# A speech joint kernel: prompts' products split around the first convolution, and transposes of the first chunk and of four weights moved from TensorE to DMA

## The chip, the cores and the metric

One core of one Trainium2 chip runs the kernel. The metric is the device time of one execution in microseconds (us). Before the change three runs took 842.79, 841.05 and 825.72 us, the median being 841.05. A profiled execution of the same kernel is read below.

## The reference

Forward and backward pass of a small speech model with a joint network. Two batches of 16000 rows of 256 channels go through two strided convolutions with three taps, each followed by a GELU; eight prompts per batch (`g`) are projected; every remaining frame is joined with every prompt by a tanh, and the result is projected again.

```python
h = gelu(conv3(x, w1))[:, ::2, :]          # 16000 -> 8000 rows
f = gelu(conv3(h, w2))[:, ::2, :]          # 8000 -> 4000 rows
fe = jnp.einsum("btd,de->bte", f, w_f)
ge = jnp.einsum("bud,de->bue", g, w_g)
j = jnp.tanh(fe[:, :, None, :] + ge[:, None, :, :])
out = jnp.einsum("btud,dv->btuv", j, w_o)
```

The outputs are `out` and the gradients of all seven inputs (x, w1, w2, g, w_f, w_g, w_o) for a given `grad_out` of shape (2, 4000, 8, 256). All tensors are bfloat16.

## The kernel before

The 4000 frames of both batches, with a gap of 16 between them, make one line of 8016 columns that is cut into 16 chunks of 512 (`G`, the last one shorter). Channels lie on the 128 partitions, in two halves (`KT`). For each chunk n there are:

- `conv_units(n)` (L302): the first convolution. Six matmuls of 512 columns (L324) make one of its four units, ACT copies the result out of PSUM (L327), and the GELU with its derivative is spread over ACT and DVE (L264, L269). `conv2_units(n)` (L342, matmuls L359) is the second convolution; `fe_units(n)` (L374, L383, L385) makes the tile `FE`, of which there is one buffer.
- `tanh(n, u)` (L394): ACT makes `JT`, the joint of chunk n with prompt u, from `FE` and the bias `GE` (L401).
- `joint_units(n, up)` (L675), one step for a pair of prompts. `gj` multiplies the transposed output gradient `GOT` with `WOT` (L635), ACT squares JT (`JSQ`, L627), and DVE combines both to `NGZ` (L639), which POOL adds up over the prompts (`ngfe_acc`, L658). Then `o_block` projects JT with `WO` (L695) and ACT copies the output rows (L697). The gradient of w_o, `gwo` (L734), needs JT with frames on the partitions: the tile `JR`. A step runs `gwo` for the pair before it.
- the backward units of chunk n - 1: `d1_units` reads `WFT` (L431), `d5_units` reads `W2T` (L454), `e_units` reads `W1T` (L590); they are transposed weights. `WGT` is read only at the end (L910).

`JR` comes in two ways. For chunks 1 to 15, `load_jr` (L660) starts a transposing DMA from JT in SBUF (L667). For chunk 0 it only takes the buffer, and `jr_block` (L670) makes it in `joint_units`: four transposes of 128 x 128 on TensorE for each of four blocks (L467), and one DVE copy out of PSUM each (L469).

All other transposed loads (`x` in L164, `GOT` in L174, `FR` in L474) are DMAs on SP's queue too, beside the plain loads `GO` (L202) and the weights. POOL's queue writes the outputs and loads the rows of x.

Before the loop over the chunks, the start runs 16 dummy matmuls (`warm`, L782) on a tile of zeros, then `small_units` (L786), which transposes the prompts (L790) and makes `GE` (L796, L798) one batch after the other, then the convolution of chunk 0, two units of chunk 1's, three units of `transposed_units` (L801: WOT, WFT, WGT), the second convolution, the rest of chunk 1's first convolution, and the six other transposed weights (L813 on TensorE, L814 on DVE). 

`weave` (L747) sets the order in which units are written down: after every unit of a step it draws `ratio` units of a second list, the fill. In chunk 0 `ratio` is 0.4, and the fill holds the second convolution of chunk 1 and its `FE`, with empty units between. A planner then makes one list for each engine and each DMA queue from the program, its dependencies and its own idea of durations, so an instruction may come earlier than its place in the program when nothing holds it. `tc.add_manual_dep(..., NOSYNC)` puts one instruction behind another in that plan without a wait on the chip; `tc.keep_in_program_order` forbids the move. In the trace SP issues the x loads of chunk 2 (second half) and chunk 3 (first half) together at 28.99, although the latter is written down in chunk 1.

Of the kernel before, what the change touches and what calls it, by code (L numbers as in the profile page):

```python
# [22 lines left out]
P = 128  # L23
KT = 2
KK = 3
# [7 lines left out]
def kernel(  # L33
# [106 lines left out]
    W1T = const.tile([P, KK, KT, D], BF16, name="W1T")  # L140
    W2T = const.tile([P, KK, KT, D], BF16, name="W2T")
# [13 lines left out]

    def load_x(n, pairs=(0, 1)):
        W = geom(n)[1]
        for c in pairs:
            t = X1[c] if n == 1 else xcp.tile([P, 2, KT, CW + 16], BF16, name="XC")
            back = 16 * c  # L160
            for lo, hi in gaps(n, back):
                nc.vector.memset(t[:, :, :, 16 + lo:16 + hi], 0.0)
            for b, q, col, w in segs(n, back):
                nc.sync.dma_start_transpose(out=t[:, :, :, 16 + col:16 + col + w].rearrange("p c k w -> p (c k) w"),  # L164
                                            in_=xq[b, c, q:q + w, :])
            for j in range(2):
                S[n]["X", 2 * c + j] = t[:, j]
# [269 lines left out]
    def d5_units(n):  # L437
# [10 lines left out]
        for par, taps in ((0, ((1, 0),)), (1, ((2, -1), (0, 0)))):  # L448
            for mt in range(KT):
                ps = ps_f32()  # L450
                k, last = 0, len(taps) * KT - 1
                for (i, sh) in taps:
                    for kt in range(KT):
                        nc.tensor.matmul(ps[:, :N], lhsT=W2T[:, i, kt, mt * P:(mt + 1) * P],  # L454
                                         rhs=GF[:, kt, 2 + sh:2 + sh + N], start=(k == 0), stop=(k == last))
                        k += 1
                gh = nc.vector.tensor_tensor(out=GH[:, par, mt, 2:2 + N], in0=ps[:, :N],
                                             in1=G1[:, par, mt, 2 - par:2 - par + N], op=ALU.mult)
                while held:
                    tc.add_manual_dep(held.pop().ins, gh.ins.name, NOSYNC, reason="held")  # L460
                yield
# [111 lines left out]
    def e_units(n):  # L573
# [5 lines left out]
        def gx_block(k, M):  # L579
            t = gxp.tile([P, 4, D], BF16, name="GX")  # L580
            combos = (((0, 1, 0), (2, 0, -1)), ((1, 1, 0),), ((2, 1, 0), (0, 0, 0)), ((1, 0, 0),))
            for cp in range(2):
                ps = ps_f32()
                for cj in range(2):
                    cc = combos[2 * cp + cj]
                    j, last = 0, len(cc) * KT - 1
                    for (i, par, sh) in cc:
                        for kt in range(KT):
                            o = 2 + k + sh
                            nc.tensor.matmul(ps[:M, cj * D:(cj + 1) * D], lhsT=GH[:, par, kt, o:o + s * (M - 1) + 1:s],  # L590
                                             rhs=W1T[:, i, kt, :], start=(j == 0), stop=(j == last))
# [68 lines left out]
    def load_jr(n, up):  # L660
# [4 lines left out]
        if n == 0:  # L665
            return
        nc.sync.dma_start_transpose(out=JR[:].rearrange("p u k a d -> p (u k a) d"),  # L667
                                    in_=S[n]["JTP", up][:].rearrange("p u k w -> p (u k w)"))

    def jr_block(n, up, k):  # L670
        o, M = blocks(geom(n)[1])[k]
        srcs = [(S[n]["JT", 2 * up + j][:, kt, o:o + M], 2 * j + kt, M) for j in range(2) for kt in range(KT)]
        transposes(srcs, [(S[n]["JR", up][:M, :, :, k].rearrange("p u k d -> p (u k) d"), M, 0, 4)])

    def joint_units(n, up):  # L675
# [7 lines left out]
        if n == 0:  # L683
            for k in range(len(bl)):
                jr_block(n, up, k)
                yield
# [99 lines left out]
    def small_units():  # L786
        for b in range(B):
            gt = ps_bf()
            for kt in range(KT):
                nc.tensor.transpose(out=gt[:, kt, 0:U], in_=GR8[:, b, kt * P:(kt + 1) * P], identity=ident[:U, :U])  # L790
            gT = gxp.tile([P, KT, U], BF16, name="gT")
            nc.vector.tensor_copy(out=gT[:], in_=gt[:, 0:KT, 0:U])
            ge = ps_f32()
            for mt in range(KT):
                for kt in range(KT):
                    nc.tensor.matmul(ge[:, mt * U:(mt + 1) * U], lhsT=WG[:, kt, mt * P:(mt + 1) * P], rhs=gT[:, kt, :],  # L796
                                     start=(kt == 0), stop=(kt == KT - 1))
            nc.vector.tensor_copy(out=GE[:, b].rearrange("p k u -> p (k u)"), in_=ge[:, 0:KT * U])  # L798
            yield

    def transposed_units():  # L801
        jobs = []
        for WT_, W_ in ((WOT, WO), (WFT, WF), (WGT, WG)):
            jobs.append(([W_[:, dt, kp * P:(kp + 1) * P] for kp in range(KT) for dt in range(KT)],
                         WT_[:].rearrange("p k d -> p (k d)")))
        for WT_, W_ in ((W2T, W2), (W1T, W1)):
            for i in range(KK):
                jobs.append(([W_[:, i, dt, kp * P:(kp + 1) * P] for kp in range(KT) for dt in range(KT)],
                             WT_[:, i].rearrange("p k d -> p (k d)")))
        for srcs, dst in jobs:  # L810
            ps = ps_bf()
            for j, src in enumerate(srcs):
                nc.tensor.transpose(out=ps[:, j, :], in_=src, identity=ident[:])  # L813
            nc.vector.tensor_copy(out=dst, in_=ps[:, 0:4, :].rearrange("p k d -> p (k d)"))  # L814
            yield
# [7 lines left out]
    conv1, turned = conv_units(1), transposed_units()  # L823
    for _ in chain(warm(16), small_units(), conv_units(0), islice(conv1, 2), islice(turned, 3), conv2_units(0)):
        pass
# [7 lines left out]
    for n in range(G):  # L833
# [16 lines left out]
        for up in range(U // 2):  # L850
# [7 lines left out]
            for piece in (((0,), (1,), (2, 3), ()) if n == G - 1 else ((0, 1), (2, 3), (), ()))[up] if back else ():  # L858
                load_xr(n - 1, piece)
            main = joint_units(n, up)  # L860
# [95 lines left out]
```

## Time and profile before

| | before |
|---|---|
| profiled execution | 824.49 us |
| its span, first to last instruction | 822.4 us |
| granted TensorE clock, mean over the span | 0.996 |
| PE busy | 799.5 us, 97% |
| DVE busy | 627.8 us, 76% |
| ACT busy | 678.8 us, 83% |
| POOL busy | 403.4 us, 49% |
| moved by DMA | 187.88 MB, 228 GB/s |
| chain that ended last | PE 84%, ACT 8%, DVE 5% |

PE is TensorE's matmuls, DVE VectorE, ACT ScalarE, POOL GpSimd, SP SyncE. A stage line gives the start and end of the stage, its length, then the busy time of PE, PE's weight loads, DVE, ACT and POOL with the count of instructions in parentheses, the granted clock of TensorE as a share of full speed, the busy share of the 16 DMA engines (over 1 where packets overlap), and GB/s. A group line gives source line, engine, operation, output and inputs with shapes and the count, then busy time and the mean of one in ns, then the idle time of the engine just before them and what ended it. A wait line says who waited for whom: total us, times, longest. A line on DMA issues gives output and input, queue, kind, count, size, and the median us from issue to landing.

### The profile page before, as it was taken

Reading aid. Unit: us, or ns where it says so; the run is one execution under the profiler, and the core shown is the slowest. Engines: PE = TensorE matmul, PEld = TensorE weight load, DVE = VectorE, ACT = ScalarE, POOL = GpSimd, SP = SyncE. Lnnn points to the kernel's source line nnn. Section 1 sums busy time; section 2 is a strip of 40 time slices with the busy share of each in tenths; the row PEclk is TensorE's granted clock in tenths of the full one; section 3 lists DMA queues with packets and bytes.
Section 4 is the critical chain, followed back from the end, with each engine's and each line's share of the span. In section 5 each row is a group of like instructions: output and inputs, shape, how many; then the busy total and the mean of one; then the engine's idle time right before and its main releaser. Section 6 shows DMA issues by size and latency. Waiting matters only on the chain.

```text
span 822.4 us, 16555 instructions
## 1 busy us (share of the span) xinstructions
PE 799.5 (97%) x6292; PEld 596.6 (73%) x6368; DVE 627.8 (76%) x1211; ACT 678.8 (83%) x1080; POOL 403.4 (49%) x423
## 2 busy tenths in 40 slices
PE   8789999999999999999999999999999999999997
PEld 3356777868678687776767778686786867878796
DVE  3996786886869778697877968868697786968744
ACT  4988898896979969799797988969799697987744
POOL 1154644454545534544487544545455345455671
PEclk9999999999999999999999999999999999999999
DMA  9968999999999999999999999999999999999954
GB/s 216 214 172 189 212 258 236 235 220 240 260 270 207 237 229 228 261 231 203 250 232 243 248 225 252 221 250 264 262 222 241 229 241 230 211 200 249 275 135 139
DMA packets 395344, 187.88 MB, mean 228 GB/s; under 512 B 343296, under 2 KB 379032, under 8 KB 395264
## 3 DMA queue, kind: packets, MB, share of 16 engines
q1 hardware_dynamic: 374944, 119.69, 78.2%
q0 software_dynamic: 20320, 67.12, 27.0%
q8 instruction: 50, 0.82, 0.4%
q14 instruction: 30, 0.25, 0.1%
HBM read 51.38 MB, written 50.34 MB: 124 GB/s over the span
## 4 chain that ended last, share of the span: by engine, by line
PE 84%; ACT 8%; DVE 5%; issue 2%; DMA 1%; POOL 0%; POOLq 0%; DVEq 0%; ACTq 0%
PE GWO_ps L734 12%; PE ps L695 11%; PE ps L635 10%; PE ps L590 10%; PE ps L603 10%; PE ps L324 8%; PE ps L530 5%; PE pst L467 5%; PE ps L454 4%; PE ps L359 4%; ACT JT L401 2%; ACT OUT L697 2%; ACT JSQ L627 2%; PE ps L512 2%; PE ps L431 1%
## 5 line engine op out<-in xcount | busy, mean ns | idle before, releaser
L658 POOL TENSOR_TENSOR ACCN<-ACCN,NGZ 128x1024 f32<-128x1024 f32 (+1 forms) x80 | 169.1, 2114 | 74.0 <-DVE NGZ L639 73.0
L639 DVE SCALAR_TENSOR_TENSOR NGZ<-JSQ,ps 128x512 bf16<-128x512 bf16 (+3 forms) x272 | 168.6, 640 | 42.4 <-PE ps L635 32.5
L401 ACT ACTIVATE JT<-FE,GE 128x512 bf16<-128x512 f32 (+3 forms) x272 | 176.9, 707 | 0.5
L697 ACT CAST OUT<-ps 128x512 bf16<-128x512 f32 (+1 forms) x252 | 145.9, 593 | 35.2 <-PE ps L695 35.1
L627 ACT ACTIVATE JSQ<-JT 128x1024 bf16<-128x1024 bf16 (+1 forms) x128 | 134.9, 1058 | 37.2 <-DVE NGZ L639 37.2
L695 PE MATMUL ps<-WO,JT 128*128 128x256 bf16 (+1 forms) x1008 | 148.4, 272 | 2.5 <-DVE NGZ L639 2.1
L734 PE MATMUL GWO_ps<-GO,JR 128*128 128x256 bf16 (+1 forms) x1008 | 149.0, 272 | 0.7
L722 POOL DMA_DIRECT2D out_dram<-OUT x76 | 56.0, 737 | 168.4 <-ACT OUT L697 156.2
L635 PE MATMUL ps<-GOT,WOT 128*128 128x512 bf16 (+1 forms) x482 | 133.1, 374 | 2.4 <-DVE JR L469 0.9
L734 PEld LDWEIGHTS <-JR 128*128 128x128 bf16 (+1 forms) x1008 | 97.1, 98 | 26.1 <-issue 0.5
L695 PEld LDWEIGHTS <-JT 128*128 128x128 bf16 (+1 forms) x1008 | 97.4, 98 | 23.3 <-issue 3.6
L590 PE MATMUL ps<-W1T,GH 128*128 128x256 bf16 (+2 forms) x756 | 100.4, 273 | 0.7
L590 PEld LDWEIGHTS <-GH 128*128 128x128 bf16 (+2 forms) x756 | 83.5, 116 | 13.0
L603 PE MATMUL ps<-rows,XR 128*128 128x256 bf16 (+1 forms) x756 | 90.4, 273 | 0.0
L415 DVE TENSOR_TENSOR ACC<-ACC,ps 128x512 f32<-128x512 f32 x90 | 61.5, 685 | 37.5 <-PE ps L530 25.9
L264 DVE SCALAR_TENSOR_TENSOR g_s<-g_sq,g_x 128x1024 bf16<-128x1024 bf16 (+2 forms) x35 | 67.4, 1925 | 27.0 <-ACT g_sq L264 27.0
L324 PE MATMUL ps<-XC,W 128*128 128x512 bf16 (+1 forms) x359 | 86.9, 380 | 0.7
L603 PEld LDWEIGHTS <-XR 128*128 128x128 bf16 (+1 forms) x756 | 73.9, 98 | 11.6
L593 ACT CAST GX<-ps 128x512 bf16<-128x512 f32 (+2 forms) x126 | 72.2, 587 | 9.7 <-PE ps L590 5.8
L245 POOL DMA_DIRECT2D out_dram<-GX x67 | 36.9, 550 | 81.3 <-ACT GX L593 79.8
L635 PEld LDWEIGHTS <-WOT 128*128 128x128 bf16 x512 | 48.2, 98 | 34.7 <-issue 3.5
L324 PEld LDWEIGHTS <-W 128*128 128x128 bf16 x384 | 37.9, 99 | 39.2 <-issue 2.2
(133 smaller groups left out, 1228.1 us busy)
## 6 DMA issues: line engine op xcount, KB each, us to landing
GO<-in_grad_out_dram SPq DMA_DIRECT2D x56, 512.0 KB, 6.1
out_dram<-OUT POOLq DMA_DIRECT2D x56, 512.0 KB, 6.0
out_dram<-GX POOLq DMA_DIRECT2D x55, 256.0 KB, 5.1
XR<-in_x_dram POOLq DMA_DIRECT2D x39, 256.0 KB, 7.1
XR<-in_x_dram POOLq DMA_DIRECT2D x13, 320.0 KB, 7.2
GO<-in_grad_out_dram SPq DMA_DIRECT2D x4, 384.0 KB, 4.7
out_dram<-OUT POOLq DMA_DIRECT2D x4, 384.0 KB, 5.6
GOT<-in_grad_out_dram SPq DMA_TRANSPOSE x68, 7.8
```

The costliest lines, as they stand in the source:

```text
L324: nc.tensor.matmul(ps[:, :W], lhsT=W1[:, i, kt, mt * P:(mt + 1) * P], rhs=st["X", c][:, kt, 16 + sh:16 + sh + W], start=(k == 0), stop=(k ...
L401: act = nc.scalar.activation(out=JT[:, mt, lo:hi], in_=S[n]["FE"][:, mt, lo:hi], func=ACT.Tanh, bias=GE[:, b, mt, u:u + 1], scale=1.0)
L590: nc.tensor.matmul(ps[:M, cj * D:(cj + 1) * D], lhsT=GH[:, par, kt, o:o + s * (M - 1) + 1:s], rhs=W1T[:, i, kt, :], start=(j == 0), stop=( ...
L593: nc.scalar.copy(out=t[:M, 2 * cp:2 * cp + 2, :], in_=ps[:M, :])
L603: nc.tensor.matmul(ps[:, dt * D:(dt + 1) * D], lhsT=XR[:M, 4 * k + i + 2 * (1 - par), dt * P:(dt + 1) * P], rhs=t[:M, g + 2 * par:g + 2 * ...
L627: jsq = nc.scalar.activation(out=JSQ[:, :, :W], in_=JT[:, :, :W], func=ACT.Square)
L635: nc.tensor.matmul(ps[:, :W], lhsT=WOT[:, kt, mt * P:(mt + 1) * P], rhs=GOT[:, kt, :W], start=(kt == 0), stop=(kt == KT - 1))
L639: nc.vector.scalar_tensor_tensor(out=NGZ[:, mt, lo:hi], in0=JSQ[:, mt, lo:hi], scalar=1.0, in1=ps[:, lo:hi], op0=ALU.subtract, op1=ALU.mul ...
L658: st["last"] = nc.gpsimd.tensor_tensor(out=out, in0=in0, in1=st["NGZ", u][:, :, :W], op=ALU.add)
L695: nc.tensor.matmul(ps[:M, j * V:(j + 1) * V], lhsT=st["JT", u][:, kt, o:o + M], rhs=WO[:, kt, :], start=(kt == 0), stop=(kt == KT - 1))
L697: nc.scalar.copy(out=OUT[:M, k, :], in_=ps[:M, :])
L734: nc.tensor.matmul(GWO_ps[:, dt, :], lhsT=JR[:M, j, dt, k, :], rhs=GO[:M, k, j * V:(j + 1) * V], start=(n_gwo[0] == 0), stop=(n_gwo[0] == ...
```

## The change

1. `small_units` becomes `prompt_units`: its first unit transposes the prompts of both batches into one PSUM tile and copies them out at once; its second makes all of `GE`. The start now runs 12 dummy matmuls, the first unit, 9 dummy matmuls, the convolution of chunk 0, and only then the second unit.
2. `load_jr` starts the transposing DMA for chunk 0 too; `jr_block` and its units in `joint_units` are gone.
3. `transposed_units` keeps `WOT` alone. `WFT`, `W2T`, `W1T` and `WGT` are loaded from HBM by four transposing DMAs (`load_transposed`), written down ahead of the fourth step of chunk 0. W1T and W2T change their layout so that one DMA fills each.
4. `behind` orders SP's queue: the x load of chunk 2 (second half) comes behind the JR load of step 0; that of chunk 3 (first half) and the four weights come behind the JR load of step 2.

```diff
+    def behind(dma, up):
+        tc.add_manual_dep(dma.ins, S[0]["JRD", up].ins.name, NOSYNC, reason="behind the first chunk's tanh rows")
+
...
-                nc.sync.dma_start_transpose(out=t[:, :, :, 16 + col:16 + col + w].rearrange("p c k w -> p (c k) w"),
+                dma = nc.sync.dma_start_transpose(out=t[:, :, :, 16 + col:16 + col + w].rearrange("p c k w -> p (c k) w"),
                                             in_=xq[b, c, q:q + w, :])
+                if (n, c) in ((2, 1), (3, 0)):
+                    behind(dma, 0 if n == 2 else 2)
...
         S[n]["JR", up] = JR
-        if n == 0:
-            return
-        nc.sync.dma_start_transpose(out=JR[:].rearrange("p u k a d -> p (u k a) d"),
+        S[n]["JRD", up] = nc.sync.dma_start_transpose(out=JR[:].rearrange("p u k a d -> p (u k a) d"),
                                     in_=S[n]["JTP", up][:].rearrange("p u k w -> p (u k w)"))
...
-        if n == 0:
-            for k in range(len(bl)):
-                jr_block(n, up, k)
-                yield
...
+    def prompt_units():
+        gt = ps_bf()
         for b in range(B):
             for kt in range(KT):
-                nc.tensor.transpose(out=gt[:, kt, 0:U], in_=GR8[:, b, kt * P:(kt + 1) * P], identity=ident[:U, :U])
+                nc.tensor.transpose(out=gt[:, b * KT + kt, 0:U], in_=GR8[:, b, kt * P:(kt + 1) * P], identity=ident[:U, :U])
+        gT = gxp.tile([P, B * KT, U], BF16, name="gT")
+        nc.vector.tensor_copy(out=gT[:], in_=gt[:, 0:B * KT, 0:U])
+        yield
...
+    def load_transposed():
+        for WT_, w_ in ((WFT, w_f), (W2T, w2), (W1T, w1), (WGT, w_g)):
+            if WT_ in (W2T, W1T):
+                dma = nc.sync.dma_start_transpose(out=WT_[:].rearrange("p k i d -> p k (i d)"), in_=w_.rearrange("i a d -> (i a) d"))
+            else:
+                dma = nc.sync.dma_start_transpose(out=WT_[:], in_=w_)
+            behind(dma, 2)
...
-    for _ in chain(warm(16), small_units(), conv_units(0), islice(conv1, 2), islice(turned, 3), conv2_units(0)):
+    for _ in chain(warm(12), islice(prompts, 1), warm(9), conv_units(0), prompts, islice(conv1, 2), islice(turned, 3),
+                   conv2_units(0)):
...
+            if n == 0 and up == 3:
+                load_transposed()
             main = joint_units(n, up)
```

## The prediction

> **What bounds the kernel now.** I read the busy time by stage first, since a mean over the span mixes a start with a long steady stage.
>
> ```profile
> core 0: us, PE busy (x) PEld busy (x) DVE busy (x) ACT busy (x) POOL busy (x), PEclk, DMA share, GB/s
> 0.00:10.00 10.00, 6.59 (x24) 2.58 (x25) 1.25 (x7) 1.49 (x2) 3.27 (x13) 1.00 0.91 194
> 10.00:20.00 10.00, 9.84 (x46) 4.39 (x47) 5.36 (x16) 6.52 (x13) 0.00 (x0) 0.83 1.06 234
> ...
> 30.00:40.00 10.00, 6.88 (x47) 3.99 (x47) 9.97 (x23) 9.68 (x16) 1.90 (x2) 1.00 1.04 231
> 40.00:50.00 10.00, 8.77 (x67) 5.79 (x67) 10.00 (x21) 9.15 (x15) 5.70 (x6) 1.00 0.45 113
> 50.00:60.00 10.00, 7.16 (x57) 4.96 (x57) 10.00 (x18) 8.45 (x14) 6.87 (x4) 1.00 0.71 186
> 60.00:70.00 10.00, 8.84 (x67) 5.82 (x67) 7.92 (x22) 7.90 (x12) 5.11 (x4) 1.00 0.61 175
> 70.00:810.00 740.00, 735.25 (x5867) 558.26 (x5936) 570.40 (x1076) 620.93 (x989) 377.41 (x391) 1.00 1.09 233
> ```
>
> From 70 to 810 us PE is busy 735.25 of 740. The change removes nothing there: all its edits lie in the first 70 us or are loads. So what it can win is the distance by which that full stage starts earlier, and what it can lose is a new hole at its start. In 30 to 70, PE is busy 31.65 of 40 and DVE 37.9, with ACT at 35.2. The chain of waits through these 40 us alternates between ACT and DVE, mostly ACT (JT, JSQ, OUT). DMA has room in 40 to 70 (0.45, 0.71, 0.61 against 1.09 later).
>
> Second, finer stages around the first convolution, for the granted clock:
>
> ```profile
> 8.00:9.40 1.40, 0.01 (x1) 0.00 (x0) 0.17 (x1) 0.00 (x0) 0.00 (x0) 1.00 1.07 183
> 9.40:10.40 1.00, 0.68 (x11) 0.58 (x12) 0.32 (x3) 0.00 (x0) 0.00 (x0) 0.90 1.28 291
> 10.40:13.60 3.20, 3.20 (x9) 1.09 (x8) 0.16 (x1) 0.60 (x2) 0.00 (x0) 0.50 0.99 214
> 13.60:20.00 6.40, 6.35 (x35) 3.09 (x35) 5.14 (x14) 5.92 (x12) 0.00 (x0) 1.00 1.08 240
> ```
>
> PE is empty from 8.0 to 9.4 (the prompts' products wait for WG), and the clock is 0.50 from 10.4 to 13.6, exactly under the first convolution.
>
> Third, the waits of ACT from 24 to 70 us, the groups of DVE and PE that go, and the landings:
>
> ```profile
> ACT OUT L697 <- PE ps L695: 2.9, 2, 2.0
> ACT g_s L264 <- DVE g_s L264: 1.9, 2, 1.5
> ```
> ```profile
> L469 DVE COPY JR<-pst 128x512 bf16<-128x512 bf16 x16 | 5.9, 410 | 0.0
> L467 PE MATMUL pst<-ident,JT 128*128 128x128 bf16 x64 | 5.2, 218 | 3.6 <-DVE NGZ L639 3.3 <-DVE JR L469 0.3
> ```
> ```profile
> JR<-JT SPq DMA_TRANSPOSE x60, 7.2
> ...
> WG<-in_w_g_dram POOLq DMA_DIRECT2D x1, 128.0 KB, 6.1
> ...
> GR<-in_g_dram POOLq DMA_DIRECT2D x1, 8.0 KB, 4.3
> ```
>
> ACT is idle only 4.8 us of these 46, all of it behind work that the change takes away or that stands in one line with it.
>
> **Part 1, prompts around the convolution.** The 16 dummy matmuls start at 1.81; 12 go at 0.427 us each (their weight loads stand that far apart), to 6.9, the other four at the full rate. Now 12 run, to 6.9; GR is issued at 2.66 and lands 4.3 later, at 7.0; four transposes take some 0.2 us; nine dummies at 0.216 (the pitch after 13.6) take 1.9. The convolution starts at about 9.2 instead of 10.20. Its x: the second pair is issued at 2.2 and lands 7.5 later, at 9.7, before its taps are due; the first pair's landing has no record, at latest 10.2, so the earlier start is worth 0 to 1.0. PE has no hole of 1.4 us before it any more, so I expect clock 1.0: eight matmuls that lie between 10.2 and 13.6 at 0.427 would take 0.216, another 1.7. The first unit ends at 9.2 + 6 x 0.216 = 10.5 and its cast starts at 10.6 instead of 12.96: 2.4 earlier. From there ACT is nearly dense to the first tanh (28.78), so I carry 2.4, between 0.7 (x late, one dummy too many) and 2.7. The moved products (8 small matmuls, about 0.5 us) run behind the convolution, while ACT and DVE make the GELU; GE is needed only at the tanh, 11 us later. Without that cover they would cost 0.5.
>
> The Trainium skill ("TensorE: Matmul & The Clock Gate", Part 1) says that the clock halves after an idle window of about 3.4 us and rises after a busy one. Here a hole of 1.4 us was enough, as the 0.50 row shows, so the measurement decides; by the page's rule no hole this short would matter, the earlier start alone would be left, 1.0 instead of 2.4 us, and the sum would read 821.0.
>
> **Part 2, first chunk's JR by DMA.** Gone are 64 transposes on PE (0.056 apart: 3.6 us) and 16 copies on DVE (0.41 long, 0.33 apart: 5.3 us). PE has holes there, so its 3.6 buy little by themselves; but in each of the four steps the output matmuls L695 stand behind these transposes, which stand behind DVE (3.6 us of waits), and ACT waits 2.9 for L695. Added: four JR transposes on SP. The bound is ACT's own idle time, 4.8 us (2.9 + 1.9); DVE gives back more than that with Part 3. Nothing of the rest of ACT's work is removed. I take 3.0 of the 4.8, because POOL's additions stretch DVE instructions beside them (a 0.68 us multiply took 2.06 at 38.91, 2.56 at 46.64) and will go on doing so; the ends are 0 and 4.8.
>
> The new wait: SP waits for the tanh of both prompts, and behind it in its queue stand GOT, GO and x. GOT has cover: those issued at 50.67 and 61.39 are used by L635 only 20 us later. JR itself is needed by L734. Before, the last tanh of steps 0, 1, 2 ends at 31.9, 40.5, 47.8, and L734 reads at 42.8, 53.1, 62.1: 10.9, 12.6 and 14.4 us. The steps shorten by 1 to 2, so 9 is left at worst, against landings of 4.3 to 12.3, median 7.2: hidden, with 2 us of cover. The fourth JR is read a whole step later.
>
> **Part 3, four weights by DMA.** Gone are 32 transposes on PE (1.8 us) and 8 DVE copies (2.6 at 0.33), six of them between 30.5 and 32.9, just ahead of the NGZ that everything waits for. Their worth is inside the 4.8. Added are 1.05 MB on SP behind the third JR, some 45 to 55 us; WFT is first read at 71.4, W2T at 77.5, W1T at 96.7, WGT at the end. Hidden by 10 us and more.
>
> **Load on DMA.** Two 512 KB transposes back to back took 6.44 us from 17.11: 163 GB/s. Four JR and the weights are 3.1 MB, 19 us of transposing. Room in 40 to 70 against the 1.09 later: 6.4 + 3.8 + 4.8 = 15 us, and x for chunk 3 is put off by 3. So it about fits, and some lag is passed into the steady stage; its transfers have 10 to 20 us of cover. I charge nothing, between 0 and 5.
>
> **Part 4, weaving.** A step of the first chunk has 12 units instead of 16; at 0.4 it draws 4 fill units instead of 6. FE of chunk 1, drawn in the third step before, comes after the fourth now. Then FE copies, JT and JSQ (1.0 + 2.5 + 1.0 by ACT's pitches) stand between the last outputs and the first NGZ of chunk 1, while PE has L635 and three convolution units of its own, 5.6 us. I charge 0.5, between 0 and 4.5.
>
> **Sum.** 2.4 + 3.0 - 0.5 = 4.9. The profiled execution took 824.49 us, 2.1 more than its span: 822.4 - 4.9 = 817.5, **819.6 us**. The three runs shown are 842.79, 841.05 and 825.72; the profiled one is like the lowest, and no row explains the 2.1% between them. If the changed kernel's median lies where the upper two do, this reads 819.6 x 841.05 / 824.49 = 836.1.
>
> **Rivals.**
> - *Everything pays*: 2.7 + 4.8 + 0.8 for two copies in front of the first tanh: 816.2. For it: ACT's waits name just these lines. Against: DVE stays stretched by POOL.
> - *Given back at chunk 1*: FE is late, the 4.5 us of Part 4 are all exposed, and nothing is won: about 824. For it: ACT is 10.00 busy from 70 to 80, so late ACT work is not made up. Against: seven PSUM buffers let PE run ahead by 5.6 us.
> - *JR late, slower than before*: the place is L734 in steps 1 to 3. JR comes in a queue with weights, GOT and GO; if it lands as the latest did (12.3) with 9 us of cover, PE stands for 3.3 us three times: 819.6 + 9.9 = 829.5. It decides from a landing of 9 us on. For it: the first JR loads in the trace land latest, and PE's order is fixed. Against: DMA is at half load there. The Trainium skill ("VectorE: DVE Perf Modes", The three transpose paths) speaks for it: 390 ns for a 128x128 tile on TensorE, 1309 by DMA; 16 tiles in line would take 21 us, an estimate from that page, missing the cover by 12. The trace disagrees: 7.2 us for 16 tiles is 0.45 each.
> - *The clock gains nothing*: GR is late, a hole stays, Part 1 is worth 0.7: 821.3. It is in the forecast's own range.
>
> **Chances.** Forecast (817 to 822) 0.52; everything pays 0.10; given back 0.20; JR late 0.18. All four lie within 2%, which is about what a measurement of this kernel can tell from no change. A bigger change can come only from the unexplained 2.1% between runs or from another order of the steady stage: faster by over 2% 0.10, within 0.82, slower 0.08. Range: from 816.2 less 3 for another order, 813, to the forecast's upper end at the upper runs' level, 822 x 1.02, 838.
>
> **What would show it.** Right: clock 1.00 from 9.5 on with the first L324 before 9.6; first L327 near 10.6 and first JT near 26.4; no L469 on DVE before 65; ACT's idle time from 24 to 65 under 2 us; JR landing in 9 us; PE over 99% from 65 on. Wrong: a wait of PE on JR or on W2T, a clock of 0.50 under L324, or ACT idle at the first FE of chunk 1. A steady stage longer than 740 us for the same work would overturn the whole argument.

## The result and the profile after

The changed kernel is slower: 840.84 us (six executions, 835.71 to 848.58) against 839.38 for the kernel before beside it (six, 822.31 to 861.63). The ratio is 1.0114 [1.0068, 1.0159], some 9.4 us; a second measurement gave 1.0102 [1.0029, 1.0175]. A ratio compares the medians of executions without a disturbance, so it is not the quotient of the two medians above. The profiled execution took 839.92 us, its span is 837.9.

From 100 to 200 us hardly anything has changed; in the first 100 us, which I call the head, much has. The stages of the changed kernel, columns as before:

```profile
core 0: us, PE busy (x) PEld busy (x) DVE busy (x) ACT busy (x) POOL busy (x), PEclk, DMA share, GB/s
0.00:10.00 10.00, 6.20 (x21) 2.30 (x22) 1.01 (x5) 1.49 (x2) 3.26 (x13) 0.92 0.89 199
...
30.00:40.00 10.00, 4.65 (x23) 2.14 (x24) 10.00 (x19) 10.00 (x17) 7.35 (x6) 0.78 1.15 236
40.00:50.00 10.00, 9.95 (x63) 6.44 (x62) 5.30 (x13) 6.70 (x12) 4.96 (x3) 0.88 0.83 209
50.00:60.00 10.00, 6.67 (x46) 4.31 (x46) 6.29 (x12) 9.22 (x15) 4.95 (x3) 0.98 1.13 206
60.00:70.00 10.00, 9.28 (x45) 4.93 (x44) 6.55 (x13) 8.72 (x15) 7.04 (x7) 0.85 1.07 240
70.00:80.00 10.00, 1.85 (x9) 1.34 (x10) 2.54 (x9) 1.24 (x2) 2.48 (x2) 0.66 1.17 229
80.00:100.00 20.00, 19.47 (x145) 13.11 (x144) 12.12 (x21) 18.17 (x27) 7.61 (x10) 0.91 1.08 210
100.00:200.00 100.00, 99.47 (x784) 74.61 (x793) 78.37 (x139) 89.28 (x139) 48.01 (x47) 1.00 1.07 234
```

From 100 on PE is busy 99.5%, as before. But from 30 to 40 it is busy 4.65 us instead of 6.88, and from 70 to 80, where the kernel before was already full, 1.85. The clock, 1.00 in the same rows before, is 0.78, 0.88, 0.98, 0.85 and 0.66 between 30 and 80. From 40 to 70 DMA's share has gone from 0.45 to 0.83, from 0.71 to 1.13 and from 0.61 to 1.07: from 50 us on it is as high as it was in the steady stage (1.09). The waits of PE say for what, total, times, longest:

```profile
PE GWO_ps L728 <- DMA JR<-JT: 19.6, 5, 8.8
PE pst L784 <- DMA GR<-in_g_dram: 2.0, 1, 2.0
```

In the profile before, PE had no wait on JR at all. L728 is `gwo` here, L689 the output products, L640 the products with GOT. In the chain of work that ended last, the pieces on DMA (start, length) are now

```profile
2.65 5.38 DMA GR<-in_g_dram
...
33.53 4.96 DMA JR<-JT
51.95 6.29 DMA JR<-JT
66.78 11.32 DMA JR<-JT
552.22 8.20 DMA JR<-JT
772.37 15.00 DMA JR<-JT
```

The three JR in the head end in waits of 3.7, 3.3 and 8.8 us, 15.8 together; the two late ones in 0.5 and 3.3. As a marker for the head I take the first matmul that reads `W1T`, the first gradient of x: it starts at 106.0 us, before at 96.7. Those 9.3 us are as much as the measured difference. That is partly chance: the two spans differ by 15.5, so 6.2 came behind the marker, and in a second pair of profiles the marker stands at 100.7 and 94.4 (experiment 8).

**Why the readers stand.** The first wait of PE on JR, in order of time (start, length, count, and in brackets the idle time before):

```profile
33.60 0.60 PE L689 MATMUL ps<-WO,JT 128*128 128x256 bf16 x4 [1.17 <-DVE NGZ L644]
34.21 0.59 PE L640 MATMUL ps<-GOT,WOT 128*128 128x512 bf16 x2
38.54 0.39 PE L728 MATMUL GWO_ps<-GO,JR 128*128 128x256 bf16 x1 [3.74 <-DMA JR<-JT]
```

PE comes to the first `gwo` product at 34.8; before, it did so at 42.8. With the sixteen transposes of a step gone, the planner fills PE's holes with `gwo`: by the order of time, 13 of the 16 products of this pair stand ahead of the next outputs, where 4 did. L640, which DVE's next work needs, stands behind it in PE's list and goes on only at 38.73. The second wait is on the JR of step 2, for which PE is ready at 55.0 instead of 62.1. The third wait, on the JR of step 3, is made on SP's queue (start, length of the issue):

```profile
51.95 3.12 SPq L670 DMA_TRANSPOSE JR<-JT  x1
55.13 1.60 SPq L811 DMA_TRANSPOSE WFT<-in_w_f_dram  x1
56.78 1.48 SPq L809 DMA_TRANSPOSE W2T<-in_w_dram  x1
58.36 1.33 SPq L207 DMA_DIRECT2D GO<-in_grad_out_dram  x1
59.74 4.02 SPq L809 DMA_TRANSPOSE W1T<-in_w_dram  x1
63.80 1.27 SPq L811 DMA_TRANSPOSE WGT<-in_w_g_dram  x1
65.17 1.51 SPq L179 DMA_TRANSPOSE GOT<-in_grad_out_dram  x1
66.78 5.11 SPq L670 DMA_TRANSPOSE JR<-JT  x1
```

The last tanh of step 3 ends at 59.75, its JR is issued at 66.78, behind W1T, WGT and GOT, and lands 11.3 later at 78.1. From 51.95 to 71.89 the queue issues with no pause of more than 0.1 us. PE has been idle since 69.3; it used to come to these products at 74.5.

### The profile page after: what moved, and what is told of

Same layout as the page of the kernel before. It is cut to its first block, busy times and chain, and to the rows that moved or that the text cites. A ratio compares the mean times of both kernels' runs of the same rounds, so it can differ in the third digit from the quotient of the medians.

```text
span 837.9 us, 16361 instructions
## 1 busy us (share of the span) xinstructions
PE 801.3 (96%) x6202; PEld 594.3 (71%) x6277; DVE 616.1 (74%) x1185; ACT 678.2 (81%) x1080; POOL 412.5 (49%) x423
## 4 chain that ended last, share of the span: by engine, by line
PE 84%; ACT 7%; DMA 6%; DVE 2%; issue 1%; POOL 0%; POOLq 0%; DVEq 0%; ACTq 0%
PE GWO_ps L728 12%; PE ps L689 12%; PE ps L640 10%; PE ps L595 9%; PE ps L608 9%; PE ps L329 8%; DMA JR<-JT 5%; PE ps L535 5%; PE pst L472 5%; PE ps L364 4%; PE ps L459 4%; ACT JT L406 2%; PE ps L517 2%; PE ps L436 1%; ACT OUT L691 1%
## 5 line engine op out<-in xcount | busy, mean ns | idle before, releaser
L728 PE MATMUL GWO_ps<-GO,JR 128*128 128x256 bf16 (+1 forms) x1008 | 151.7, 276 | 20.3 <-DMA JR<-JT 19.6
L689 PE MATMUL ps<-WO,JT 128*128 128x256 bf16 (+1 forms) x1008 | 152.2, 276 | 2.5 <-DVE NGZ L644 1.2
L640 PE MATMUL ps<-GOT,WOT 128*128 128x512 bf16 (+1 forms) x482 | 134.0, 377 | 0.2
L728 PEld LDWEIGHTS <-JR 128*128 128x128 bf16 (+1 forms) x1008 | 98.2, 99 | 49.8 <-DMA JR<-JT 22.0
L689 PEld LDWEIGHTS <-JT 128*128 128x128 bf16 (+1 forms) x1008 | 98.3, 99 | 25.3 <-ACT JT L406 2.9
L640 PEld LDWEIGHTS <-WOT 128*128 128x128 bf16 x512 | 48.4, 98 | 32.0 <-issue 0.7
```

The lines of the kernel that those rows point to most:

```text
L640: nc.tensor.matmul(ps[:, :W], lhsT=WOT[:, kt, mt * P:(mt + 1) * P], rhs=GOT[:, kt, :W], start=(kt == 0), stop=(kt == KT - 1))
L689: nc.tensor.matmul(ps[:M, j * V:(j + 1) * V], lhsT=st["JT", u][:, kt, o:o + M], rhs=WO[:, kt, :], start=(kt == 0), stop=(kt == KT - 1))
L728: nc.tensor.matmul(GWO_ps[:, dt, :], lhsT=JR[:M, j, dt, k, :], rhs=GO[:M, k, j * V:(j + 1) * V], start=(n_gwo[0] == 0), stop=(n_gwo[0] == ...
```

## The experiments

The theory at the outset: the first two waits come from readers placed early, the third from weights ahead of JR in the queue. The rivals: one of the two alone, or no wait but what the transfers cost elsewhere. "Head" is the time of the marker above in the one profiled execution of each run; ratios are to the kernel before on the same chip.

**1. Weights on TensorE as before, the rest of the change kept (`e1_no_weights`).**

```diff
-            if n == 0 and up == 3:
-                load_transposed()
# and transposed_units makes all nine tiles on TensorE again; W1T and W2T keep the changed layout
```

> All of the change but the four weights, which TensorE transposes as before. Theory Q (the queue: JR of step 3 left SP only at 66.8 us, seven us after its tanh, because four weight loads and a GOT stood ahead of it): the 8.8 us wait of PE near 70 us is gone or under 2 us, the two earlier JR waits (3.7 and 3.3) stay, the half clock after 70 is gone, and the time falls by 8 to 12 us against the changed kernel, to about the kernel before. Rival T (transposing JR by DMA is too slow for a 10 us step, whatever stands ahead): the wait near 70 stays above 5 us, and the time falls by under 3 us.

Measured 1.0033 [0.9979, 1.0088], head 102.0. The wait near 70 us is gone; at 39 and 54 PE still waits 0.6 and 4.3 for JR. So the third wait belongs to the weights. The head also holds a wait of 3.1 us for GR at its start, which has nothing to do with JR.

**2. Weights behind the fourth JR (`e2_weights_behind_jr3`).**

```diff
-            behind(dma, 2)
+            behind(dma, 3)
```

> The changed kernel with the four weight loads planned behind the JR load of step 3 instead of that of step 2; the loads themselves are the same. Theory Q: JR of step 3 is issued at about 60 to 61 and lands by 68, so its wait is under 2 us; WFT leaves SP after it and PE may wait for WFT instead, 0 to 4 us; the time falls by 4 to 10 us against the changed kernel. Rival T: JR of step 3 still lands 10 us and more after its issue, the wait stays above 5 us, the time falls by under 3 us.

Measured 1.0116 [1.0072, 1.0161], head 102.4. The wait for the fourth JR is gone, as expected, but PE now waits 2.0 for `WFT`, and the first two waits on JR are 7.7 and 3.5. Against the changed kernel the ratio has not moved, where 4 to 10 us were expected: turning the queue round pays nothing here.

**3. JR on TensorE, weights by DMA (`e3_jr_on_pe`).**

```diff
+        if n == 0:
+            return
         S[n]["JRD", up] = nc.sync.dma_start_transpose(...)
# jr_block and its units as before; the weights come behind step 3's load of GO; the x loads are not ordered
```

> All of the change but JR of chunk 0, which TensorE transposes as before (x loads unordered again); the weights still come by DMA, behind the GO load of step 3. Theory Q and rival T both say that no wait of PE on JR is left before 100 us and the clock stays 1.00 from 13 us on. If the weights by DMA are harmless when nothing urgent is behind them, the time is 822 to 826, the before's or 1 to 3 us under it; if they load the DMA engines so that other transfers come late, PE waits elsewhere and it is 3 us over it or more.

Measured 1.0022 [0.9971, 1.0073], head 92.5, the shortest of all, with no wait on JR before 100. The four weights by DMA do the head no harm alone: it is 2 to 4 us shorter than in the two profiles of the kernel before. The total does not follow: behind 250 us there are eight waits on JR, 14.1 us in all.

**4. The prompts' split alone (`e4_front_only`, again as `e18_front_again`).** The kernel before with `prompt_units` and the new order of the start.

> The kernel before with the prompts' products split around the first convolution, and nothing else. In the changed kernel the convolution started at 11.9 instead of 10.2 (GR landed 5.4 us after its issue, PE stood for 2.0, and nine dummies ran at half clock), but at the full clock, and the first tanh came at 29.3 against 28.8. Theory: this part is worth nothing to within 1.5 us either way, no wait on JR, time 822 to 827. Rival, my forecast's Part 1: 2.4 us under the kernel before.

> The kernel before with the prompts' split alone, a second time: it measured 0.9889 [0.9831, 0.9948], which its first 100 us (95.2 against 96.7 and 94.4 us in two executions of the kernel before) do not explain. Theory: the split is worth the 0 to 1.5 us that its head shows, so the ratio is 0.995 to 1.002 and the first measurement was among late and early transfers of the later stage. Rival: it is a gain of some 1% again, 0.983 to 0.994, and the version beats both kernels.

First 0.9889 [0.9831, 0.9948], then 1.0023 [0.9955, 1.0092], heads 95.2 and 95.1. The gain did not repeat. An interval from one session does not hold all that varies from session to session here, so every ratio near 1% below is to be read with that in mind.

**5. `gwo` without JR (`e5_before_gwo_free`, `e6_after_gwo_free`).** In the kernel before and in the changed one, the product reads `WOT`, a tile that has long been there, in place of JR; the gradient of w_o is not computed.

```diff
-  nc.tensor.matmul(GWO_ps[:, dt, :], lhsT=JR[:M, j, dt, k, :], rhs=...
+  nc.tensor.matmul(GWO_ps[:, dt, :], lhsT=WOT[:M, dt, j * P:(j + 1) * P], rhs=...
```

> The kernel before, but the w_o gradient's matmuls read the weight tile WOT in place of JR; all JR transposes and copies still run, the matmuls have the same shapes, and that one output is not the gradient. No PE instruction waits for JR any more. Theory J (the spread of 2 to 3% between runs of one kernel, 822 to 853, is PE waiting for late JR loads in the steady stage, as in the later profiles at 400 to 560 and near 787 us): all runs lie between 815 and 826, the spread falls under 8 us and the median is about 820. Rival (the spread has another cause, for instance the clock): the median stays at 830 to 838 and the spread above 15 us.

> The changed kernel with the same substitution as the run before it: no wait on JR, all loads kept. Theory Q and J together: the first e_units matmul, at 106.0 in the changed kernel and 96.7 in the kernel before, comes at 90 to 93, as the forecast's 4.9 us of gain says, and the median is 814 to 819, 3 to 6 us under the run without JR waits of the kernel before. Rival (the change loses in the head by something other than JR, such as FE drawn late or DMA load): the first e_units matmul stays after 96, and the median is not below the other's.

Measured 0.9965 [0.9918, 1.0012] and 1.0117 [1.0002, 1.0232]. In the kernel before the executions still spread from 821 to 838 us, so late JR is not what spreads them, or not alone. In the changed kernel no reader waits for JR now, yet no gain is seen, though the interval is too wide to rule one out. In the profiled execution, the longest of four (850.94 us), PE waits 22.5 us for GO and 5.4 for GOT, the longest 9.3 at 82 us. There JR was only the tile of SP's queue that was asked for first.

**6. `gwo` two steps late (`e7_before_gwo_two_steps`, `e8_after_gwo_two_steps`).** A third buffer of JR, for which one of JT's four went.

```diff
-    jtp = pool("jtp", 4)
+    jtp = pool("jtp", 3)
...
-    jrp = pool("jrp", 2)
+    jrp = pool("jrp", 3)
...
-    prev_gwo = [None]
+    prev_gwo = [None, None]
# and GO is loaded one step later, and two pairs are left for the end
```

> The kernel before with the w_o gradient run two steps behind instead of one (three JR buffers, three JT buffers instead of four, GO loaded one step later); nothing is left out. Theory J: JR has some 22 us instead of 11, so hardly any PE wait on JR is left; the median falls to 818 to 826 and the spread under 10 us. Rival: the median stays within 4 us of the kernel before.

> The changed kernel with the same two-step distance: nothing left out. Theory Q and J: JR waits in the first chunk vanish (they were 3.7, 3.3 and 8.8), first e_units matmul at 90 to 95, median 812 to 822 and below the kernel before with the same distance by 1 to 6 us. Rival T (DMA transposes of the first chunk and the weights overload the queue whatever the distance): waits on JR above 5 us stay before 100 us, and it is not below the other.

Measured 1.0215 [1.0012, 1.0418] and 1.0255 [1.0171, 1.0338]. Both are slower, against the expectation, and they tell nothing on the question. In the first kernel L695 stands 14.1 and 6.2 us for ACT; the 14.1 end behind a JR load that was issued at 777.85 and took 21.6 us. That the missing buffer of JT ties ACT to this load is likely, but not shown. In the second the planner placed `gwo` early all the same, with JR waits of 2.8, 3.4 and 7.8 in the head.

**7. `gwo` of chunk 0 held in program order (`e9_pinned`, `e10_pinned_weights_late`).** The second also has edit 2.

```diff
+                if n == 0:
+                    tc.keep_in_program_order(mm)
```

> The changed kernel, but the w_o gradient's matmuls of chunk 0 are kept at their place in the program on PE; in the changed kernel's plan they stand up to 3 us of PE work earlier, in holes (10 of 16 ahead of the second step's outputs, 9 of 16 ahead of the fourth's, one block ahead of chunk 1's first outputs). DMAs and their order are the same. Theory P (the planner takes JR to land sooner than it does, and PE, which runs its list in order, stands at the matmul put too early): the first two JR waits fall from 3.7 and 3.3 to under 1 us each, the third from 8.8 to 3 to 7, the first e_units matmul comes at 96 to 101 instead of 106.0. Theory Q (only what stands ahead of JR in SP's queue counts): the waits move but their sum stays above 12 us, first e_units matmul after 103.

> Both: the matmuls of chunk 0 kept at their place, and the four weight loads behind the JR load of the fourth step. Theories P and Q together: JR waits before 100 us are under 2 us in all, WFT may cost 0 to 3, the first e_units matmul comes at 91 to 96, at or under the kernel before's 96.7, and the time is 0 to 6 us under the kernel before. If DMA in the first 70 us is simply overloaded (theory T), waits on JR, GO, GOT or WFT above 6 us in all stay there.

Measured 1.011 [1.0029, 1.0191] and 1.0081 [1.0026, 1.0136]; heads 96.0 and 99.2. In the first, PE comes to the first `gwo` product at 38.99, both early waits are gone and one of 3.4 at 72 us is left. In the second no wait on JR comes before 100, and PE's waits read

```profile
PE ps L436 <- DMA WFT<-in_w_f_dram: 5.9, 1, 5.9
PE GWO_ps L728 <- DMA JR<-JT: 4.6, 3, 3.1
```

So the early placement made the first two waits: shown. That they were the loss is not shown: without them the ratio stays, though its four executions leave 0.3 to 1.9%.

**8. Both kernels once more (`e11_before_again`, `e12_after_again`).**

> The kernel before once more, for a second look. The first e_units matmul comes again at 96 to 98 us, without a wait on JR ahead of it. Theory J (in the steady stage JR, and the loads beside it, land late at random, in every kernel): if this execution is above 828 us, the rest is in PE waits on DMA or behind it after 100 us; the lucky profile of before, 822.4, had none.

> The changed kernel once more. Its head repeats: three JR waits before 80 us of 3 to 4, 3 to 4 and 7 to 10 us, half clock after the third, the first e_units matmul at 104 to 108; the time is 1.005 to 1.016 of the kernel before.

The kernel before, one execution: 839.13 us, head 94.4. Its chain has

```profile
393.71 5.72 DMA GO<-in_grad_out_dram
610.07 16.73 DMA JR<-JT
...
768.76 17.80 DMA JR<-JT
```

with waits of PE on JR of 5.4 and 6.1 us. From the head to the end it took 742.7 us, where the execution I had predicted from took 725.7. The changed kernel: ratio as given above, head 100.7 where 104 to 108 was expected, JR waits of 4.0, 3.2 and 4.1 in the head.

**9. Fewer stores, in the kernel before (`e13_fewer_stores`) and in the changed one (`e14_changed_fewer_stores`).** Some 12 MB of stores of the gradient of x are left out in chunks 2 to 13. If the added transfers cost in the steady stage, room there should hide them.

```diff
     def store_gx(n, k, t):
+        if 2 <= n <= 13:
+            return
```

> The kernel before, with the stores of GX (the gradient of x) left out for chunks 2 to 13: some 48 of the 55 stores of 256 KB, about 12 of 188 MB, so that part of one output is not written. Nothing on any other engine changes. Theory D (the steady stage is bound by TensorE and by the transfers nearly alike: the 3 to 6 us waits of TensorE for tanh rows near 500, 630 and 787 us, and the spread of 822 to 861 us between executions, are transfers that come late, and whatever adds transfers anywhere lengthens them): with 6% less to move the waits for tanh rows total under 3 us in the profile, and the median falls by 0.5 to 1.5%, to 826 to 833 us. Rival R (the steady stage is bound by TensorE alone and only the first 100 us decide): within 0.3% of the kernel before.

> The changed kernel with the same stores left out, part of one output not written. Its first 100 us are those of the changed kernel, with 3 MB more on the queue and 7 to 15 us of waits for tanh rows there. Theory D: with slack in the transfers of the steady stage, nothing is added behind the first 100 us, and what stays against the run without those stores is what the first 100 us lose: 4 to 9 us, 0.5 to 1.1%. Rival T (the loss of the changed kernel is paid in the steady stage by the added transfers, and the loss of the first 100 us is otherwise made good there): within 0.3% of the run of the kernel before without those stores.

Measured 0.9977 [0.9948, 1.0006] and 1.0107 [1.0069, 1.0144]: 829.35 us (826.99 to 832.23) and 838.52 (835.24 to 841.26), 9.2 apart, with no overlap. The mean granted clock of single executions lies between 0.989 and 0.997 for the first and between 0.981 and 0.987 for the second. The DMA pieces in the first one's chain:

```profile
3.28 7.25 DMA WG<-in_w_g_dram
...
763.72 16.82 DMA JR<-JT
```

and in the second's:

```profile
2.65 7.34 DMA GR<-in_g_dram
34.95 4.82 DMA JR<-JT
53.03 12.05 DMA JR<-JT
70.45 7.00 DMA JR<-JT
103.68 5.82 DMA JR<-JT
770.49 14.47 DMA JR<-JT
```

PE's waits on these five JR are 3.3, 8.8, 1.6, 1.0 and 3.0 us. Behind 110 us both are alike: PE busy 700.65 and 702.91 of 710 us, the second without a wait on JR until 785. The heads end at 98.1 and 103.3, and behind them the two profiled executions took 732.3 and 730.7. So with room in the steady stage the loss stays, and what these two profiles show of it, 5.2 us, lies in the head: Rival T, that it is paid in the steady stage, falls. The profiled execution of the first was its longest, which is why the two spans differ by 3.6 only and not by 9.2.

**10. As many bytes added, but in the steady stage (`e15_added_loads`).** The kernel before with 24 loads of 128 KB behind JR loads in chunks 1 to 12.

```diff
+        jr = nc.sync.dma_start_transpose(...)    # the JR load, as it was
...
+        if n <= 12 and up % 2 == 0:
+            t = extra.tile([P, CW], BF16, name="EXTRA")
+            x = nc.sync.dma_start_transpose(out=t[:], in_=grad_out[...])
+            tc.add_manual_dep(x.ins, jr.ins.name, NOSYNC, reason="behind the tanh rows")
```

> The kernel before, with 24 added transposing loads of 128 KB (3.1 MB in all, as many bytes as the change adds) from the gradient into a spare tile that nobody reads, two in each of chunks 1 to 12, each put on SP's queue right behind a transfer of tanh rows. The first 60 us are those of the kernel before. Theory D: 3.1 MB in the steady stage cost about what 3.1 MB cost the changed kernel, +0.5 to +1.2%, with waits for tanh rows of 10 to 20 us in the profile after 100 us. Rival R (only the first 100 us decide): within 0.3% of the kernel before.

Measured 1.0271 [1.0219, 1.0323], more than expected: 22 us for 24 loads, 0.9 us each. The head is untouched (96.3), the waits are late ones:

```profile
294.67 7.36 DMA JR<-JT
317.62 7.68 DMA JR<-JT
350.51 5.96 DMA JR<-JT
485.09 13.12 DMA JR<-JT
638.08 11.34 DMA JR<-JT
681.45 9.07 DMA JR<-JT
782.95 16.08 DMA JR<-JT
```

So transfers added to SP's queue are not free in the steady stage either; "only the first 100 us decide" is wrong as a rule. Bytes alone are not the price: 3.1 MB cost 9 us in the head and 22 in small pieces here, while 12 MB fewer stores, which go by another queue, gained 0.2%, an interval that holds no change.

**11. The split with the prompts' rows first on POOL's queue (`e16_front_prompts_first`).**

```diff
+    nc.gpsimd.dma_start(out=GR8[:], in_=g.rearrange("b u d -> u b d"))   # moved ahead of this load:
     nc.gpsimd.dma_start(out=W1[:], ...)
```

> The kernel before with the prompts' products split around the first convolution as in the change, and nothing else of the change, and the prompts' rows loaded first on POOL's queue, ahead of the first convolution's weights, so that they land before the twelve dummy products end. Theory: the 2 us wait for the prompts' rows goes, the clock stays full under the first convolution, which starts 1 to 3 us earlier than in the changed kernel if its own weights do not come later than 10 us; median 0.3 to 1.3% under the kernel before (the split alone measured 0.9889). Rival: the first convolution's weights land later behind the added load, or the start is worth nothing that lasts, and the ratio is within 0.4% of 1.

Measured 1.0049 [0.9999, 1.01], head 104.0. The rival's mechanism held, and its bound of 0.4% was just missed. The wait on GR is gone, and the convolution waits 8.4 us for its weights:

```profile
2.48 14.44 DMA W<-in_w_dram
```

In the kernel before this load landed 5.4 us after its issue. The run changed nothing ahead of it but a load of 8 KB.

**12. Split and JR by DMA, pinned, without the weights (`e17_pinned_no_weights`).** Edits 1 and 7 together.

> The changed kernel with the weights transposed on TensorE as before, and L728's products of chunk 0 held in program order on TensorE: of the change only the prompts' split and the tanh rows by transfer are left, without the early placing of their readers and without weights in the queue. Theory (the loss is made of waits in the first 100 us: early readers, and the weights ahead of the last rows of chunk 0; the rows by transfer themselves cost nothing): no wait for tanh rows before 100 us, the first gradient of x begins by 96 us against 102 with the readers left early and 94 to 97 in the kernel before, and the ratio is 0.988 to 1.000. Rival (1 MB more on the queue costs by itself, since the transfers bound the later stage nearly as TensorE does): the first 100 us are as short, but the ratio stays at 1.002 to 1.010.

Measured 0.9973 [0.9900, 1.0045], head 98.2 with one wait on JR of 2.2 us before 100, where I had expected none. Within the interval the total is that of the kernel before.

## Why the prediction was wrong

**The cause, as far as the runs go.** No part alone shows a loss that is clear of the noise: the split 0.9889 and 1.0023, and each with the split, rows by DMA 1.0033, rows with pinned readers 0.9973, weights by DMA with the rows on TensorE 1.0022. Rows and weights together, in whatever order and with readers pinned or not, gave 1.0114, 1.0116, 1.011, 1.0081 and 1.0102, each with an interval above 1. The intervals of the parts reach up to 0.9% and 0.7%, so it is not shown that the two lose more together than their parts added up.

Where the changed kernel loses is better known. In three profiles of it (one with fewer stores) the head ends at 106.0, 100.7 and 103.3, in three of the kernel before at 96.7, 94.4 and 98.1: 6.9 us apart in the mean. From there to the end it took 731.9, 736.0 and 730.7 against 725.7, 742.7 and 732.3, no longer in the mean. In the head PE stands for whichever tile is last: JR, WFT, GO or GOT. Early placement and the order of the queue decide which tile that is. That the two moves together are too much for SP's queue there is a reading that fits, but it is not shown: DMA's share from 50 to 80 us is 1.12 in the changed kernel, but also 1.07 in `e3_jr_on_pe` and 1.12 in `e17_pinned_no_weights`, whose ratios show no loss, and no run gave that queue more room.

**Part 2 is the step that failed**: "hidden, with 2 us of cover". I took the time of L734's first read, 42.8, from the kernel before. But `gwo` stood there because PE had transposes to do ahead of it; the same edit that made its input later made it earlier, to 34.8. Of the 9 us of cover, 2.9 were left, counted from the end of the tanh at 31.9 as I did. The landings were as forecast, 5.0 and 6.3 in the first two waits. I should have asked where the planner puts a reader whose neighbours are gone, and had written myself that an instruction comes earlier when nothing holds it.

**Load on DMA, "I charge nothing", failed too.** I had 19 us of transposing against 15 of room, and then let the lag be hidden by the cover of Part 2. The 19 were too sure as well: the 163 GB/s behind them came from how long SP issued two transfers, and in the same profile the issue of one JR of 512 KB took from 1.6 to 6.1 us. Part 3's weights, "hidden by 10 us and more", were: WFT is there before its reader. They paid through the JR behind them, which I had put ahead: "the fourth JR is read a whole step later" left out that it is also issued 7 us after its tanh. I counted the cover of the moved transfers, not of those queued behind them.

**Part 1 was mis-sized: 2.4, in truth about nothing.** I took GR's landing as 4.3 us, from a single row, and it took 5.4; and the twelve dummy products, which I had ending at 6.9, ended at 6.1. PE was empty between and the clock fell all the same:

```profile
6.20:8.20 2.00, 0.12 (x4) 0.13 (x4) 0.00 (x0) 0.00 (x0) 0.00 (x0) 1.00 1.15 279
8.20:11.90 3.70, 3.70 (x14) 1.36 (x13) 0.17 (x1) 0.00 (x0) 0.00 (x0) 0.54 1.09 221
```

The nine dummy products ran at half speed, then the clock rose again, and the convolution began at 11.9 instead of 9.2, at full clock. First cast 13.4 (10.6 forecast), first JT 29.3 (26.4). So the hole was moved, from WG's wait to GR's. The kernel before in its second profile waited only 0.7 for WG, and had the full clock from 6 to 18 with the old order:

```profile
6.00:18.00 12.00, 11.01 (x61) 5.07 (x60) 5.49 (x17) 6.33 (x12) 0.00 (x0) 1.00 1.12 243
```

Its first JT came at 26.9. The half clock that I had counted as this kernel's property was that of one execution.

How long PE waits does not decide it. Waits of 1.4, 2.0 and 3.1 us at this place (before, after, `e1_no_weights`) were followed by half clock, and so was one of 1.1 (`e15_added_loads`); waits of 0.7 and 1.2, but also of 1.7 (`e2_weights_behind_jr3`) and 2.0 (`e5_before_gwo_free`), were not. The clock records of the twenty profiles show what does. Every stretch at full or half clock but the last of a profile lasts a whole number of steps of 3.41 us. Up to 820 us, half clock followed each of the 56 full-clock steps in which PE was busy for 43% or less, and none of those with 53% or more; of the 21 steps between, it followed 7. The 1.4 us of the kernel before lie in one step, which is busy to 50%, and half clock follows. The 2.0 us of `e5_before_gwo_free` are cut by the end of a step, so that both steps are busy to 57% and more, and the clock stays (first line before, the others that run):

```profile
6.79:10.20 3.41, 1.71 (x17) 0.87 (x16) 0.47 (x3) 0.00 (x0) 0.00 (x0) 1.00 1.22 262
...
5.10:8.51 3.41, 1.94 (x9) 0.69 (x7) 0.00 (x0) 0.00 (x0) 0.00 (x0) 1.00 1.25 241
8.51:11.93 3.42, 2.16 (x19) 1.26 (x20) 0.64 (x4) 0.00 (x0) 0.00 (x0) 1.00 1.06 206
```

The Trainium skill ("TensorE: Matmul & The Clock Gate", Part 1) has the clock halve after an idle window of about 3.4 us and rise after a busy one of that length, in windows that run freely. The length and the free running agree with these steps. But a step need not be idle to halve the clock: here it is enough that PE is busy for less than about half of it, and the measurement decides. So the 0.50 row, on which I had built 1.7 of the 2.4 us, hung on where in a step the hole fell.

**The base.** 824.49 us was a low draw: of 95 executions of the kernel before that were timed beside the experiments, five were at or below it, their median is 834.3, and half lie between 829.4 and 838.9. I had seen that "no row explains the 2.1%" and kept the low level as the forecast. The second profile shows a part of what is missing: JR landing 17 to 18 us after its turn near 610 and 770 us, with waits of 11.4 us in a span that is 14.7 longer. It is not the whole, since without any reader of JR (`e5_before_gwo_free`) the executions spread by 17 us all the same. My range to 838 allowed for that level, but not for it and a loss of 1%.

**The rivals.** "JR late, slower than before" named the mechanism and its engine, and had 0.18. Its price was 9.9 us of waits, measured 15.8; its condition, "from a landing of 9 us on", was wrong, since two of the three waits came with landings of 5.0 and 6.3. I had let the landing decide, and the place of the reader did. The tiles' rate, for which I had cited the Trainium skill ("VectorE: DVE Perf Modes", The three transpose paths: 1309 ns for a tile by DMA), went against the page again: 6.7 us in the median for the 16 tiles of a JR, 0.42 each; the rival's side was right for another reason. "Given back at chunk 1" has its sign too: the first FE products of chunk 1 start at 63.6, and ACT's idle time from 24 to 65 is 5.4 us, not under 2, with 4.6 of it behind L689. "The clock gains nothing" came true in its cause, GR late and a hole left, and belongs to Part 1.

**Open.** The head of one profile does not give the total: e9's head is as short as before and its ratio 1.011, e16's is 7 to 10 us longer and its ratio 1.0049. Between the markers and the totals lies the lateness of the steady stage, 725.7 to 742.7 us for the same instructions in two executions. So how the loss is shared between early readers and queue is not settled; e1 and e17 (1.0033 and 0.9973) differ by less than their intervals. No version was shown to beat the kernel before: the split's first gain did not repeat.

## What to carry to other kernels

When an edit moves a producer to DMA, look up where its reader will stand after the edit, not where it stood: work taken off an engine lets a planner pull the readers forward, just as their input becomes later. Count, for each queue, what comes to stand behind the added transfers, and add the parts up on that queue: two moves that show no loss alone can together cost 1%. And a sum of a few us made against one execution needs to know where that execution lies among many.

## What the runs showed of the hardware

- The granted clock changed only in steps of 3.41 us, and fell after a step in which PE was busy for less than about half (always at 43% and less, never at 53% and more, over the first 820 us of twenty profiles). So a hole of 1.4 us halved it where the hole lay in one step, and one of 2.0 us cut by a step's end did not. A late tile can thus cost twice, once in waiting and once in slow products: in the head of the changed kernel's profile the steps at half clock add up to 23.9 us, before to 3.4. The longer an execution took, the lower was its mean clock: over the 95 executions of the kernel before the correlation is -0.87.
- With some 230 GB/s moving, a JR transfer of the same 512 KB landed after 5 us or, in the chains above, after 17.8. Seventeen of the twenty profiles here have one that was issued between 763 and 783 us and takes 12 to 22 us in the chain; the one that I predicted from has none.
- 24 transposing loads of 128 KB, added to SP's queue in the steady stage, cost 0.9 us each (1.0271), far more, byte for byte, than the 12 MB of stores left out on POOL's queue gave back (0.9977).
